# The second layer of experts 1 to 7 by Strassen's seven block products, interleaved with those of the first layer

## The chip, the cores and the metric

The kernel runs on one core of a Trainium2 chip. The metric is the device time of one execution in microseconds; of several runs the median is given. Five engines work side by side, each through its own instructions in order: TensorE (PE), VectorE (DVE), ScalarE (ACT), GpSimd (POOL) and SyncE (SP). They meet through semaphores, which the tile framework sets wherever one engine reads or overwrites what another wrote.

## The reference

Sparse attention over B=4, H=8, S=768, D=64 (32 neighbouring keys and 24 block summaries for each query) gives x, 3072 tokens of 512 numbers. The change lies in the dense mixture of experts behind it:

```python
logits = x @ w_gate                              # N=3072, E=8
P = np.exp(logits - logits.max())
for _ in range(8):                               # Sinkhorn
    P /= P.sum(1, keepdims=True) + 1e-09
    P /= P.sum(0, keepdims=True) + 1e-09
    P *= N / E
for e in range(E):                               # D=512, F=1024
    h = np.maximum(x @ w1[e], 0.0)
    out += P[:, e:e+1] * (h @ w2[e])
```

## The kernel before

**Stage 1** (pool `attn`) computes the attention, the gate, all of expert 0 and the Sinkhorn iterations. A planner, `Plan`, lays it out: `add` gives it units of work with an engine, a cost, a priority and what they depend on, and it fixes the order in which they are issued. Expert 0 is cut into batches of half a sequence (384 tokens): eight tiles of the hidden layer (`hidden_mm`, L204, four matmuls of 384 columns each, bank `hps`), then three output tiles (`project_mm`, L209, eight matmuls of 512 columns each, bank `yps`). A Sinkhorn iteration is `sink_rows` (L492 to L496: row sums, reciprocals, multiplication, column sums, all on DVE), `sink_cols` (L502: a matmul that adds the column sums over the partitions) and `sink_apply` (L505, L506, DVE). Weights are loaded on POOL's DMA queue, `load_w1` and `load_w2`, 1 MB each and expert.

**Stage 2** (pools `fast` and `fps`) computes experts 1 to 7 in an order that is written out by hand. A step is an expert e and a slice j of 512 tokens out of each half of the 3072 (21 steps). Each step has four groups (i = 0 to 3; 84 in all).

The **first layer** of a group makes four tiles of 128 features by 512 tokens by the Strassen-Winograd scheme: two halves of features, two of the contraction, two of tokens, seven block products instead of eight. Each product is two matmuls of 512 columns (`product`, L807), with operands that are quarters of w1 (A11 to A22) and x (B11 to B22) or sums of them (S1 to S4 from `w_sum`, L787 to L796; T1 to T4 from `x_sums`, L772 to L775). p1 goes to bank `pa`, and ACT copies it to bank `pg` (L822, called the seed here); p6 adds to `pg`, p2 to `pa`. p5 goes to `pb`, and ACT copies it out (L828, c5), as it does `pg` after p6 (L833, c2). p3 adds to `pb`, p7 to `pg`, and `both` (L840, L841) adds c2 or c5 on DVE and takes the relu. p4 adds to `pg` at last. ACT takes the relu of p1+p2 and of the last state of `pg` (L195). The hidden tiles `hf` are half precision (FP16).

The **second layer** is plain: of the step before, each group makes two output tiles of 128 tokens (`out_tile`), eight matmuls of 512 columns each in a bank `yps` (L209), and DVE adds the tile times its column of P to `out_acc` (L871). For expert 1, `out_acc`, which holds expert 0's output, is first multiplied by expert 0's column of P (L860). SP stores a tile after expert 7.

So a group is 14 matmuls of the first layer and 16 of the second, all 512 columns wide, each with a weight load of its own. p4 of a group is issued only after p1 and p5 of the next (`late`). The four groups of the first step have no second layer beside them and run two at a time; the fifth group is the first of the steady part. After the last group its step's eight output tiles remain alone, 64 matmuls.

Of the kernel before, what the change touches and what calls it, by code (L numbers as in the profile page):

```python
# [113 lines left out]
def kernel(  # L114
# [38 lines left out]
    ident = const.tile([128, 128], BF16)  # L153
    ident16 = const.tile([128, 128], FP16)
    band = const.tile([128, LIVE], BF16)
    m_blk = const.tile([128, G, 64], BF16)
    col_en = const.tile([128, 128], FP32)
    warm = const.tile([1, 8], FP32)
    zeros = const.tile([128, 512], BF16)
# [11 lines left out]
    def band_constants():  # L171

        nc.gpsimd.affine_select(out=band, in_=band, compare_op=ALU.is_ge, fill=0.0,
                                base=-1, pattern=[[1, LIVE]], channel_multiplier=-1)
        nc.gpsimd.affine_select(out=band, in_=band, compare_op=ALU.is_ge, fill=0.0,
                                base=2 * W - 1, pattern=[[-1, LIVE]], channel_multiplier=1)


    w1s, w2s = {}, {}

    def load_w1(e, part=0, parts=1):
        if part == 0:
            w1s[e] = wpool.tile([128, KD, F], FP16, tag="w1", name="w1")
        fw = F // parts
        nc.gpsimd.dma_start(  # L185
            out=w1s[e][:, :, part * fw:(part + 1) * fw],
            in_=moe_w1[e].rearrange("(dk p) f -> p dk f", p=128)[:, :, part * fw:(part + 1) * fw])
# [14 lines left out]
    def hidden_mm(e, hp, t0, n, f):  # L202
        for dk in range(KD):
            nc.tensor.matmul(hp[:, 0:n], lhsT=w1s[e][:, dk, f * 128:(f + 1) * 128],  # L204
                             rhs=xT[:, dk, t0:t0 + n], start=(dk == 0), stop=(dk == KD - 1))
# [12 lines left out]
    with tc.tile_pool(name="attn", bufs=1) as attn, \  # L218
         tc.tile_pool(name="aps", bufs=1, space=PSUM) as aps, \
         tc.manual_schedule():  # L220

        qT = [attn.tile([128, W + S + W], BF16, name=f"qT{i}") for i in range(NB)]
# [268 lines left out]
        def sink_rows():  # L491
            nc.vector.tensor_reduce(out=rs_sb[:], in_=P_sb[:], axis=AX.X, op=ALU.add)  # L492
            nc.vector.reciprocal(out=rrec_sb[:, :, 0], in_=rs_sb[:])
            nc.vector.tensor_tensor(out=P_sb[:], in0=P_sb[:],
                                    in1=rrec_sb[:].to_broadcast([128, NT, E]), op=ALU.mult)
            nc.vector.tensor_reduce(out=csum_sb[:], in_=P_sb[:].rearrange("p t e -> p e t"),  # L496
                                    axis=AX.X, op=ALU.add)

        def sink_cols():

            at["sink"] = bank("a", "sink")[:, 0:E]
            nc.tensor.matmul(at["sink"], lhsT=col_en, rhs=csum_sb[:], start=True, stop=True)  # L502

        def sink_apply(last):
            nc.vector.reciprocal(out=crec_sb[:, 0, :], in_=at.pop("sink"))  # L505
            nc.vector.scalar_tensor_tensor(out=P_sb[:], in0=P_sb[:], scalar=1.0 / XS if last else 1.0,  # L506
                                           in1=crec_sb[:].to_broadcast([128, NT, E]),
                                           op0=ALU.mult, op1=ALU.mult)

        def hidden0(key, t0, f):  # L510
            if f == 0:
                at["h", key] = hpool.tile([128, KF, 512], FP16, tag="h", name="h")
            hp = at["hp"] = bank("m", "hps")
            hidden_mm(0, hp, t0, HS, f)
            return hp
# [6 lines left out]
        def keep_busy(n):  # L522

            t = bank("m", "idle")
            for _ in range(n):
                nc.tensor.matmul(t[:], lhsT=zeros[:, 0:128], rhs=zeros[:], start=True, stop=True)  # L526
# [4 lines left out]
        for t in v_x:  # L531
            nc.vector.memset(t[:, :, :, D:VD], 1.0 / XS)

# [139 lines left out]
        def expert0(t0, xs):  # L673
# [3 lines left out]
            w = [U["w1", 0], U["w1", 1]]  # L677
# [39 lines left out]
        load(("w1", 0), lambda: load_w1(0, 0, 2), 0.85, 2.5)  # L717
        load(("w1", 1), lambda: load_w1(0, 1, 2), 0.85, 2.5)
# [11 lines left out]
        for i in range(PB, NP):  # L730
# [3 lines left out]
            if i % PB == PB - 1:  # L734
# [4 lines left out]
                expert0(b * S + HS, xs)  # L739
        load("w1n", lambda: load_w1(1), 0.85, 5.0)  # L740
# [14 lines left out]
    with tc.tile_pool(name="fast", bufs=1) as fast, \  # L755
         tc.tile_pool(name="fps", bufs=1, space=PSUM) as fps, \
# [5 lines left out]
        FH = F // 2  # L762
        steps = [(e, j) for e in range(1, E) for j in range(NJ)]
        xTs = fast.tile([128, 4, KH, NH], FP16, name="xTs")
        ws = {}
        hs = {}

        def x_sums(j):
            a, b = slice(512 * j, 512 * (j + 1)), slice(NH + 512 * j, NH + 512 * (j + 1))
            lo, hi = xT[:, 0:KH, :], xT[:, KH:KD, :]  # L770
            t = [xTs[:, n, :, a] for n in range(4)]
# [111 lines left out]
        for j in range(NJ):  # L883
            x_sums(j)
# [70 lines left out]
```

## Time and profile before

| | us |
|---|---|
| three runs: median, lowest, highest | 720.6, 720.39, 722.2 |
| the profiled execution | 721.05 |
| its span in the trace | 719.3 |

The profile is of one execution, on the hardware. In the rows, "L209" is a line of the code above, "x8" so many instructions of the same kind on end, "out<-in" the tiles written and read, followed by the shape. In the chain of waits and the timeline a row starts with its time from the span's start and its length; square brackets hold the engine's idle time before it and the instruction that ended it. Matmuls are pipelined, so a row's length is more than its cost on PE, which is the distance from one start to the next. The granted clock is TensorE's, as a share of full speed (1.00 throughout here).

### The profile page before, as it was taken

What the parts mean: (1) busy time and instruction counts of PE and PEld (TensorE: products, weight loads), DVE (VectorE), ACT (ScalarE), POOL (GpSimd) and SP (SyncE); (2) the same over time, 40 slices, a digit from 0 to 9 for tenths busy, and PEclk for the clock granted to TensorE, in tenths of its full rate; (3) what the DMA queues carried; (4) which work ended last, traced back from release to release, by engine and by line L of the source; (5) the groups of instructions that cost most, each with busy time, mean ns of one, the idle gap of its engine ahead of it and who ended that gap; (6) DMA issues with size and microseconds to landing.
All of it is one profiled execution on the core that took longest, in us unless ns stands there. A gap on an engine that the chain in (4) does not pass through costs nothing.

```text
span 719.3 us, 10589 instructions
## 1 busy us (share of the span) xinstructions
PE 704.5 (98%) x4182; PEld 341.0 (47%) x4186; DVE 422.1 (59%) x922; ACT 328.6 (46%) x596; POOL 86.4 (12%) x112
## 2 busy tenths in 40 slices
PE   8999999799999999999999999999999999999997
PEld 4666665453444444444444444444444444444443
DVE  6878887852666655554555455544555455544553
ACT  4677776456434433444334433444334433444330
POOL 9599700000000000000000000000000000000000
PEclk9999999999999999999999999999999999999999
DMA  9999960007000340030301230033003120001223
GB/s 133 177 130 127 132 97 3 1 1 117 1 1 0 60 59 0 1 59 7 52 1 19 40 60 0 1 60 58 1 0 59 13 47 1 1 0 60 78 83 132
DMA packets 86609, 33.70 MB, mean 47 GB/s; under 512 B 68640, under 2 KB 79904, under 8 KB 86560
## 3 DMA queue, kind: packets, MB, share of 16 engines
q0 software_dynamic: 77968, 26.22, 33.6%
q1 hardware_dynamic: 8064, 6.80, 3.1%
q8 instruction: 33, 0.54, 0.3%
q14 instruction: 16, 0.13, 0.1%
q10 hardware_dynamic: 528, 0.02, 0.0%
HBM read 52.45 MB, written 6.29 MB: 82 GB/s over the span
## 4 chain that ended last, share of the span: by engine, by line
PE 95%; DVE 4%; issue 0%; ACT 0%; DVEq 0%
PE yps L209 46%; PE pg L807 15%; PE pa L807 10%; PE pb L807 10%; PE hps L204 5%; PE sg L297 1%; PE tkq L278 1%; PE idle L526 1%; PE ss L383 1%; PE vs L305 1%; PE tx L469 1%; PE av L431 1%; DVE hf L840 1%; PE av L369 1%; PE av L375 1%
## 5 line engine op out<-in xcount | busy, mean ns | idle before, releaser
L209 PE MATMUL yps<-w,hf 128*128 128x512 f16 x1344 | 329.4, 379 | 0.0
L871 DVE SCALAR_TENSOR_TENSOR out_acc<-yps,P_sb,out_acc 128x512 f32<-128x512 f32 x168 | 126.0, 750 | 237.4 <-PE yps L209 237.4
L209 PEld LDWEIGHTS <-hf 128*128 128x128 f16 x1344 | 131.5, 98 | 158.6
L822 ACT COPY pg<-pa 128x512 f32<-128x512 f32 x84 | 47.8, 571 | 259.9 <-PE pa L807 259.9
L807 PEld LDWEIGHTS <-ws 128*128 128x128 f16 x672 | 65.7, 98 | 79.3
L807 PE MATMUL pa<-xT,w 128*128 128x512 f16 x336 | 99.3, 379 | 0.1
L807 PE MATMUL pg<-xTs,ws 128*128 128x512 f16 x336 | 99.3, 379 | 0.0
L807 PEld LDWEIGHTS <-w 128*128 128x128 f16 x504 | 49.3, 98 | 63.6 <-issue 4.6
L833 ACT COPY c<-pg 128x512 f32<-128x512 f32 x84 | 49.1, 588 | 42.3 <-PE pg L807 42.3
L840 DVE TENSOR_TENSOR hf<-pb,c 128x512 f16<-128x512 f32 x84 | 57.2, 681 | 16.6 <-PE pb L807 16.5
L840 DVE TENSOR_TENSOR hf<-pg,c 128x512 f16<-128x512 f32 x84 | 57.4, 683 | 0.0
L195 ACT ACTIVATE hf<-pg 128x512 f16<-128x512 f32 x84 | 51.6, 614 | 9.2 <-PE pg L807 9.2
L807 PE MATMUL pg<-xTs,w 128*128 128x512 f16 x168 | 50.0, 379 | 3.5 <-DVE hf L840 3.5
L841 DVE TENSOR_SCALAR hf<-hf 128x512 f16<-128x512 f16 x168 | 49.4, 294 | 5.8
L195 ACT ACTIVATE hf<-pa 128x512 f16<-128x512 f32 x84 | 50.5, 604 | 0.0
L807 PE MATMUL pb<-xTs,ws 128*128 128x512 f16 x168 | 49.6, 379 | 0.0
L807 PE MATMUL pb<-xT,ws 128*128 128x512 f16 x168 | 49.6, 379 | 0.0
L828 ACT COPY c<-pb 128x512 f32<-128x512 f32 x84 | 49.5, 592 | 0.0
L185 POOL DMA_DIRECT2D w<-in_moe_w_dram x9 | 7.0, 786 | 353.3 <-PE pg L807 225.1
L204 PE MATMUL hps<-xT,w 128*128 128x384 f16 x256 | 47.2, 326 | 0.0
L209 PE MATMUL yps<-w,h 128*128 128x512 f16 x192 | 46.2, 379 | 0.0
L204 PEld LDWEIGHTS <-w 128*128 128x128 f16 x256 | 23.3, 99 | 15.2 <-issue 1.5
(110 smaller groups left out, 531.4 us busy)
## 6 DMA issues: line engine op xcount, KB each, us to landing
w<-in_moe_w_dram POOLq DMA_DIRECT2D x15, 1024.0 KB, 8.6
out_dram<-out_acc SPq DMA_DIRECT2D x24, 256.0 KB, 2.0
vx<-in_v_dram POOLq DMA_DIRECT2D x32, 96.0 KB, 5.1
kst<-in_k_dram POOLq DMA_DIRECT2D x24, 96.0 KB, 4.5
qst<-in_q_dram POOLq DMA_DIRECT2D x24, 96.0 KB, 4.2
w<-in_moe_w_dram POOLq DMA_DIRECT2D x2, 512.0 KB, 8.5
kst<-in_k_dram POOLq DMA_DIRECT2D x4, 192.0 KB, 4.6
qst<-in_q_dram POOLq DMA_DIRECT2D x4, 192.0 KB, 4.9
```

The source lines that it names most:

```text
L195: nc.scalar.activation(out=out, in_=in_, func=AF.Relu, bias=0.0, scale=1.0)
L204: nc.tensor.matmul(hp[:, 0:n], lhsT=w1s[e][:, dk, f * 128:(f + 1) * 128], rhs=xT[:, dk, t0:t0 + n], start=(dk == 0), stop=(dk == KD - 1))
L209: nc.tensor.matmul(yp[:], lhsT=h[:, f, c * 128:(c + 1) * 128], rhs=w2s[e][:, f, :], start=(f == 0), stop=(f == KF - 1))
L278: nc.tensor.transpose(t[:, g * 128:(g + 1) * 128], st[:, g, :, :].rearrange("p j d -> p (j d)"), ident)
L297: nc.tensor.matmul(dst, lhsT=kT[r][p0:p0 + 64, g * 128:(g + 1) * 128], rhs=qT[r][p0:p0 + 64, g * 128 + l0:g * 128 + l1], start=True, stop= ...
L807: nc.tensor.matmul(bank[:], lhsT=weight(e, a, dk, i), rhs=moving(b, dk, j), start=start and dk == 0, stop=dk == KH - 1, skip_group_check=True)
L822: nc.scalar.copy(out=G["g"][:], in_=G["a"][:])
L828: nc.scalar.copy(out=G["c5"][:], in_=G["b"][:])
L833: nc.scalar.copy(out=G["c2"][:], in_=G["g"][:])
L840: nc.vector.tensor_tensor(out=hb[:, f, :], in0=bank[:], in1=c[:], op=ALU.add)
L841: nc.vector.tensor_scalar_max(out=hb[:, f, :], in0=hb[:, f, :], scalar1=0.0)
L871: nc.vector.scalar_tensor_tensor(out=out_acc[:, t, :], in0=yp[:], scalar=P_sb[:, t, e:e + 1], in1=out_acc[:, t, :], op0=ALU.mult, op1=ALU.add)
```

## The change

**Second layer.** `pair(e, j, c)` makes the two output tiles ta (of the first half of the tokens) and tb (of the second) by seven block products as well, q1 to q7, with four matmuls of 256 columns each (`product2`, L811): the halves are those of tokens, of the 1024 features and of the 512 output columns. The bank tile `xy` holds four accumulators of 256 columns, 0 to 3. q1 goes to 0 and ACT copies it out (L918, c1); q5 goes to 1; DVE adds both into 2 (v5); q6 adds to 2 and ACT copies that to 3 (L930, v6); q2 adds to 0, q7 to 2, q3 to 3, q4 to 1. Then DVE adds 0 and 3, times P, to tile ta (ya, L948), and 1 and 2 to tile tb (yb, L948). The left half of tb is kept as a difference; `fin` undoes it for expert 7, and a POOL subtraction behind `scale0` sets it up for expert 1.

**Its operands.** The hidden tile of a group is now `hf` [128, 7, 512]: A11, A12, A22, S1, S2, S4 and one place that holds first A21 and then S3. c12 and c22 are the sums of bank and copy that `both` made (L757), r12 and r22 their relus (L866, L869), r11 and r21 the relus on ACT (L187); s1, s3, s2, s4 are four new sums on DVE (L757, L754). The sums of w2 (`w2_sum`, three tiles and one in place) are made a piece at a time; so are those of w1 (`w1_sums`, one set for each e and i, with S3 in place of A21). w1 comes in four pieces of two DMAs. T3 is made in place of part of x.

**Order.** The second layer runs four groups behind the first (`LAG = 4`). On PE a group is q1, p1, p5, q5, p2, p6, q6, p3, p7, q2, q4, q3, p4, q7. The buffers c5 and c2 go from two to one each. After the last group four pairs remain, 112 matmuls, two of them with banks of the first layer for their accumulators.

**Moved.** The Sinkhorn iterations (`sinkhorn()`) and the second half of expert 0's last batch (`rest_of_0()`) go from stage 1 into the first groups of stage 2, where `route()` and `filler()` call them. Sinkhorn's two multiplications go from DVE to POOL (L988, L1000). `scale0`, expert 0's scaling, goes from DVE to ACT (L903).

```diff
-    hpool = ctx.enter_context(tc.tile_pool(name="hpool", bufs=2))
-    mps = ctx.enter_context(tc.tile_pool(name="mps", bufs=3, space=PSUM))
...
-        prev = [U["lo", b] for b in range(B)]
-        for n in range(8):
-            rows = add("DVE", 1.65, sink_rows, prev, 0)
-            buf = Buffer("a")
-            cols = add("PE", 0.1, sink_cols, [rows], 0, opens=[buf], lag=0.1)
-            prev = [add("DVE", 0.6, lambda n=n: sink_apply(n == 7), [cols], 0, uses=[buf])]
...
+        def w2_sum(e, n):
             if n == 0:
+                ws2[e] = extra[0].tile([128, 3, FH, DH], FP16, tag="ws2", name="ws2", bufs=2)
+            m = {w: moving2(w, e) for w in "B11 B12 B21 B22 T1 T2 T3 T4".split()}
+            sub(*[m[w] for w in (("T1", "B12", "B11"), ("T2", "B22", "T1"), ("T3", "B22", "B12"),
+                                 ("T4", "T2", "B21"))[n]])
...
+        def product2(e, c, bank, a, b, start):
+            w = moving2(b, e)
+            for f in range(FH):
+                nc.tensor.matmul(bank, lhsT=a(f)[:, 128 * c:128 * (c + 1)], rhs=w[:, f, :],
+                                 start=start and f == 0, stop=f == FH - 1, skip_group_check=True)
...
+            h = hs[e, j, i] = fast.tile([128, 7, 512], FP16, tag="hf", name="hf", bufs=8)
...
+            def s1():
+                plus(h[:, S1, :], h[:, A21, :], h[:, A22, :])
+            def s3():
+                sub(h[:, S3, :], h[:, A11, :], h[:, A21, :])
+            def s2():
+                sub(h[:, S2, :], h[:, S1, :], h[:, A11, :])
+            def s4():
+                sub(h[:, S4, :], h[:, A12, :], h[:, S2, :])
...
+        def pair(e, j, c, spare=False, c1_at=None):
...
+            def scale0():
+                for t in (ta, tb):
+                    nc.scalar.activation(out=out_acc[:, t, :], in_=out_acc[:, t, :], func=AF.Copy,
+                                         scale=P_sb[:, t, 0:1])
+                nc.gpsimd.tensor_tensor(out=out_acc[:, tb, 0:DH], in0=out_acc[:, tb, DH:DM],
+                                        in1=out_acc[:, tb, 0:DH], op=ALU.subtract)
...
+            def v5():
+                plus(at(2), at(1), B["c1"])
+            def q6():
+                product2(e, c, at(2), h(S2), "T2", False)
+            def v6():
+                nc.scalar.copy(out=at(3), in_=at(2))
...
+        def sinkhorn():
+            for n in range(8):
+                nc.vector.tensor_reduce(out=rs_sb[:], in_=P_sb[:], axis=AX.X, op=ALU.add)
+                nc.vector.reciprocal(out=rrec_sb[:, :, 0], in_=rs_sb[:])
+                nc.gpsimd.tensor_tensor(out=P_sb[:], in0=P_sb[:],
+                                        in1=rrec_sb[:].to_broadcast([128, NT, E]), op=ALU.mult)
+                yield
+                nc.vector.tensor_reduce(out=csum_sb[:], in_=P_sb[:].rearrange("p t e -> p e t"),
+                                        axis=AX.X, op=ALU.add)
+                yield
+                t = fps.tile([128, 4, DH], FP32, tag="xy", name="sink", bufs=2)
+                nc.tensor.matmul(t[:, 0, 0:E], lhsT=col_en, rhs=csum_sb[:], start=True, stop=True)
+                yield
...
+            do("q1", "p1")
+            do0("r21")
+            do("c1", "seed")
+            route()
+            do0("ya", "yb")
+            do("p5", "c5")
+            filler()
+            route()
+            do("q5", "v5")
+            do0("s4", "fin")
+            do("p2", "r11")
+            if j == 2 and i > 1 and later:
+                w1_sums(e + 1, i - 2)
...
+            do("p6", "c2")
+            filler()
+            route()
+            do("q6", "v6")
+            do("p3", "c12")
+            route()
+            do("p7", "c22", "r12")
+            route()
+            do("q2", "q4", "q3")
+            filler()
+            do("r22", "s1", "s3", "p4", "s2", "q7")
+            route()
```

These are DVE's instructions of one group in the steady part of the kernel before: the two times `both`, and the accumulations of two output tiles.

```order
L840 TENSOR_TENSOR hf_4807<-pb_4865,c2_4880 128x512
L841 TENSOR_SCALAR hf_4807<-hf_4807 128x512
L840 TENSOR_TENSOR hf_4807<-pg_4863,c5_4868 128x512
L841 TENSOR_SCALAR hf_4807<-hf_4807 128x512
L871 SCALAR_TENSOR_TENSOR out_acc_83<-yps_4898,P_sb_78,out_acc_83 128x512
L871 SCALAR_TENSOR_TENSOR out_acc_83<-yps_4921,P_sb_78,out_acc_83 128x512
```

The same stretch of DVE's work in the changed kernel, from one pair's accumulations on, in a group with four w1 sums:

```order
L948 SCALAR_TENSOR_TENSOR out_acc_74<-xy_6869,P_sb_69,out_acc_74 128x512 x2
L757 TENSOR_TENSOR xy_6941<-xy_6941,c1_6950 128x256
L754 TENSOR_TENSOR hf_6868<-hf_6868 128x512
L757 TENSOR_TENSOR ws1_6970<-w1_6589 128x256
L754 TENSOR_TENSOR ws1_6970<-ws1_6970,w1_6589 128x256
L754 TENSOR_TENSOR w1_6589<-w1_6589 128x2x128
L754 TENSOR_TENSOR ws1_6970<-w1_6589,ws1_6970 128x256
L757 TENSOR_TENSOR hf_6940<-pb_6956,c2_6977 128x512
L757 TENSOR_TENSOR hf_6940<-pg_6952,c5_6959 128x512
L866 TENSOR_SCALAR hf_6940<-hf_6940 128x512
L869 TENSOR_SCALAR hf_6940<-hf_6940 128x512
L757 TENSOR_TENSOR hf_6940<-hf_6940 128x512
```

Where six instructions stood, there are now the accumulations as one row of two, the sum v5 (`xy<-xy,c1`), s4 of the group before, four w1 sums (in some groups one w2 sum, in others none), c12 and c22, two relus and s1; s3 and s2 follow behind the last row.

On ACT, these are the copies and relus of a group in the steady part of the kernel before.

```order
L822 COPY pg_4074<-pa_4071 128x512
L828 COPY c5_4079<-pb_4076 128x512
L195 ACTIVATE hf_4021<-pg_4026 128x512
L833 COPY c2_4091<-pg_4074 128x512
L195 ACTIVATE hf_4021<-pa_4071 128x512
```

The changed kernel has these on ACT in a group, from r21 of the group before on:

```order
L187 ACTIVATE hf_5017<-pg_5029 128x512
L918 COPY c1_5095<-xy_5086 128x256
L824 COPY pg_5097<-pa_5091 128x512
L832 COPY c5_5104<-pb_5101 128x512
L187 ACTIVATE hf_5085<-pa_5091 128x512
L839 COPY c2_5119<-pg_5097 128x512
L930 COPY xy_5086<-xy_5086 128x256
```

Before, c2 (`c2<-pg`) is ahead of the group's first relu (`hf<-pa`); after, that relu (r11) is ahead of c2, and c1 and v6 are new.

Last, DVE where stage 2 begins: before, the Sinkhorn rows (`rs_sb` to `crec_sb`) run among the sums of x (`xTs`).

```order
L492 TENSOR_REDUCE rs_sb_79<-P_sb_78 128x24
L772 TENSOR_TENSOR xTs_2876<-xT_77 128x2x512
L493 RECIPROCAL rrec_sb_80<-rs_sb_79 128x24
L773 TENSOR_TENSOR xTs_2876<-xT_77,xTs_2876 128x2x512
L494 TENSOR_TENSOR P_sb_78<-P_sb_78,rrec_sb_80 128x192
L774 TENSOR_TENSOR xTs_2876<-xT_77 128x2x512
L496 TENSOR_REDUCE csum_sb_81<-P_sb_78 128x8
L775 TENSOR_TENSOR xTs_2876<-xT_77,xTs_2876 128x2x512
L505 RECIPROCAL crec_sb_82<-sink_2598 128x8
```

In the changed kernel the rows of an iteration run among the first groups' sums (`hf`, `ws1`):

```order
L997 RECIPROCAL crec_sb_73<-sink_2824 128x8
L757 TENSOR_TENSOR ws1_2846<-w1_1825 128x256
L754 TENSOR_TENSOR ws1_2846<-ws1_2846,w1_1825 128x256
L754 TENSOR_TENSOR w1_1825<-w1_1825 128x2x128
L754 TENSOR_TENSOR ws1_2846<-w1_1825,ws1_2846 128x256
L986 TENSOR_REDUCE rs_sb_70<-P_sb_69 128x24
L987 RECIPROCAL rrec_sb_71<-rs_sb_70 128x24
L991 TENSOR_REDUCE csum_sb_72<-P_sb_69 128x8
L754 TENSOR_TENSOR hf_2778<-hf_2778 128x512
L997 RECIPROCAL crec_sb_73<-sink_2873 128x8
```

The multiplications of P_sb are gone from DVE's row (they are POOL's now), and between one iteration's reciprocal of `sink` and its next row sums there can stand the sums of w1 for a whole group.

More of the change, by code (lines that the diff above doesn't have):

```diff
@@ L489, in logits_out @@
                 in_=at.pop(("lp", b)), func=AF.Exp, bias=0.0, scale=1.0 / XS)
[L491 to L508, printed above, removed]
         def hidden0(key, t0, f):
             if f == 0:
-                at["h", key] = hpool.tile([128, KF, 512], FP16, tag="h", name="h")
+                at["h", key] = hpool.tile([128, KF, HS], FP16, tag="h", name="h")
             hp = at["hp"] = bank("m", "hps")
@@ L855, in group @@
[L855 to L872 removed]
+                product1(e, i, j, B["g"], "A22", "T4", False)
@@ L873, in second, with store, ya @@
                                                op0=ALU.mult, op1=ALU.add)
+            def store(t, k=slice(0, DM)):
+                nc.sync.dma_start(out=out[t * 128:(t + 1) * 128, k], in_=out_acc[:, t, k])
+            def ya():
+                add(ta, 0, 0, 3)
                 if e == E - 1:
-                    nc.sync.dma_start(out=out[t * 128:(t + 1) * 128, :], in_=out_acc[:, t, :])
-            return first, second
-        for _ in range(2):
-            t = fps.tile([128, 512], FP32, tag="g", name="pg", bufs=2)
-            nc.tensor.matmul(t[:], lhsT=zeros[:, 0:128], rhs=zeros[:], start=True, stop=True)
```

434 lines of the change are left out of this document (286 added, 148 removed).

## The prediction

> **What bounds the kernel now.** First the page's busy times, then the busy times by stretch (columns: length, then PE, PEld, DVE, ACT, POOL busy with instruction counts, granted clock, DMA share, GB/s).
>
> ```profile
> PE 704.5 (98%) x4182; PEld 341.0 (47%) x4186; DVE 422.1 (59%) x922; ACT 328.6 (46%) x596; POOL 86.4 (12%) x112
> ```
>
> ```profile
> 130.00:140.00 10.00, 7.09 (x63) 4.21 (x62) 10.00 (x25) 4.27 (x10) 0.00 (x0) 1.00 0.01 2
> ...
> 180.00:190.00 10.00, 8.25 (x39) 3.61 (x37) 6.81 (x15) 3.35 (x7) 0.00 (x0) 1.00 0.01 2
> ...
> 600.00:700.00 100.00, 100.00 (x465) 45.37 (x464) 52.75 (x98) 40.94 (x77) 0.00 (x0) 1.00 0.10 38
> ```
>
> From 190 us on PE never pauses, at full clock, while DVE works 53% and ACT 41% of the time. Before that, where attention ends and the experts begin, PE waits. The chain of waits (start, length, what) shows the period of the steady part, and PE's timeline the step of one matmul:
>
> ```profile
> 187.68 1.73 PE yps L209 x8
> ...
> 699.21 1.73 PE yps L209 x8
> 701.37 13.83 PE yps L209 x64
> ```
>
> ```profile
> 122.77 0.50 PE L469 MATMUL tx<-ident,xs 128*128 128x128 f16 x6
> 123.10 2.75 PE L209 MATMUL yps<-w,h 128*128 128x512 f16 x12
> ...
> 158.12 3.41 PE L204 MATMUL hps<-xT,w 128*128 128x384 f16 x20
> 161.37 5.34 PE L209 MATMUL yps<-w,h 128*128 128x512 f16 x24
> ...
> 166.55 0.38 PE L880 MATMUL pg<-zeros 128*128 128x512 bf16 x1
> ```
>
> A group takes (699.21 - 187.68)/79 = 6.475 us. From start to start, 24 matmuls of 512 columns take 166.55 - 161.37 = 5.18 us, 0.2158 each; 20 of 384 take 3.25 us, 0.1625 each; 6 of 128 take 0.33 us, 0.055 each. That is 0.416 ns a column and 2.6 ns a matmul, every one with weights of its own. 30 x 0.2158 = 6.474: the period is PE's issue time and nothing else.
>
> **Term 1: PE's work in a group.** 16 matmuls of 512 columns become 28 of 256; 14 stay. One of 256 columns costs 0.1625 - 128 x 0.000416 = 0.109 us. The new group is 14 x 0.2158 + 28 x 0.1092 = 6.08 us.
>
> The Trainium skill ("TensorE: Matmul & The Clock Gate", Back-to-back issue gap) says that in a real stream of loads and matmuls the step is set by both, about 81 ns at 128 columns, not 56. Its 25 ns on each narrow matmul would, as an estimate, make the group 6.08 + 28 x 0.025 = 6.78 us; the row of 55 ns at 128 columns disagrees.
>
> **Term 2: new waits in a group.** How ACT and DVE answer PE, and what they take:
>
> ```profile
> 409.40 0.59 PE L807 MATMUL pa<-xT,w 128*128 128x512 f16 x2
> 409.83 0.59 PE L807 MATMUL pb<-xTs,ws 128*128 128x512 f16 x2
> 410.08 0.57 ACT L822 COPY pg<-pa 128x512 f32<-128x512 f32 x1 [3.29 <-PE pa L807]
> 410.57 0.59 ACT L828 COPY c<-pb 128x512 f32<-128x512 f32 x1
> ```
>
> ```profile
> 130.07 0.68 DVE L788 TENSOR_TENSOR ws<-w 128x1024 f16<-128x1024 f16 x1
> 130.68 0.68 DVE L790 TENSOR_TENSOR ws<-w,ws 128x1024 f16<-128x1024 f16 x1
> ...
> 173.00 0.68 DVE L840 TENSOR_TENSOR hf<-pg,c 128x512 f16<-128x512 f32 x1
> 173.72 0.29 DVE L841 TENSOR_SCALAR hf<-hf 128x512 f16<-128x512 f16 x1
> 173.93 0.68 DVE L840 TENSOR_TENSOR hf<-pg,c 128x512 f16<-128x512 f32 x1
> ```
>
> ```profile
> 173.74 0.59 PE L807 MATMUL pg<-xTs,w 128*128 128x512 f16 x2 [1.41 <-DVE hf L840]
> ```
>
> ```profile
> L871 DVE SCALAR_TENSOR_TENSOR out_acc<-yps,P_sb,out_acc 128x512 f32<-128x512 f32 x168 | 126.0, 750 | 237.4 <-PE yps L209 237.4
> L195 ACT ACTIVATE hf<-pa 128x512 f16<-128x512 f32 x84 | 50.5, 604 | 0.0
> L195 ACT ACTIVATE h<-hps 128x384 f16<-128x384 f32 x49 | 24.0, 491 | 12.4 <-PE hps L204 11.9
> L462 DVE TENSOR_TENSOR xs<-av,rc 128x384 f16<-128x384 f32 x32 | 17.8, 558 | 1.1
> L346 DVE TENSOR_TENSOR em<-er,band 128x768 bf16<-128x768 bf16 x24 | 12.8, 550 | 1.5 <-ACT er L340 1.5
> ```
>
> ACT starts 0.25 us after the last issue of a product (409.83 to 410.08) and its next instruction 0.49 after that; PE goes on 0.06 us after the release (173.68 to 173.74). DVE instructions that don't need each other overlap by 0.08 us (0.68 long, 0.61 apart); one that needs the last starts 0.04 after it (173.68 to 173.72).
>
> PE's new group, by start: q1 0, p1 0.44, p5 0.87, q5 1.30, p2 1.74, p6 2.17, q6 2.60, p3 3.04, p7 3.47, q2 3.90, q4 4.34, q3 4.78, p4 5.21, q7 5.65. What each has to wait for:
> - p2 writes over p1's bank, so the seed copy must be out: 0.87 + 0.25 + 0.57 + 0.06 = 1.75. It is 0.01 late.
> - p7 writes over p6's bank, so c2 must be out. The relu r11 now stands ahead of it on ACT (2.18 + 0.25 = 2.43), so c2 starts at 2.92 and frees the bank at 2.92 + 0.59 + 0.06 = 3.57, where p7 is due at 3.48: 0.09 to 0.10 late, and all that is queued behind p7 with it. Before, c2 stood ahead of the relu, with projection matmuls in between, and cost nothing.
> - q6 needs v5, the new DVE sum from PSUM to PSUM. No row has one of 256 columns; 384 to 512 columns (0.558, 0.682) put it at 0.43, with 0.68 as the upper end. 1.75 + 0.25 + 0.43 + 0.06 = 2.49 against 2.61: hidden; at 0.68 q6 would be 0.13 late. Nothing suggests a gain.
> - p4 needs c22: 3.73 + 0.60 + 0.68 + 0.06 = 5.07 against 5.31, and q2 needs v6 (0.38 from the two relu rows): 3.41 + 0.38 + 0.06 = 3.85 against 4.00. Both hidden.
>
> DVE, start to start: two accumulations 0.67 each, v5 0.35, two PSUM sums 0.60, two relus 0.21 and 0.33, four half-precision sums of 512 columns 0.34 each (0.42 long, by the step from 768 to 1024 columns, 0.55 to 0.68): 4.8 us, plus 0.92 for the four first-layer weight sums or 0.61 for one second-layer sum in 8 groups of 12. That is 4.8 to 5.7 of 6.19 us: DVE is nearly full but not late. ACT has 3.1 us, and 1.0 more in the twelve groups where it now does DVE's scaling of expert 0's rows, after v6 and ahead of p4's relu, where it has room; the POOL subtraction behind it is awaited only by yb a group later. The weight loads come two groups ahead of their sums (12 us, where 1 MB lands in 8.6) on POOL, which PE does not wait for.
>
> ```profile
> w<-in_moe_w_dram POOLq DMA_DIRECT2D x15, 1024.0 KB, 8.6
> ```
>
> So a group takes 6.08 + 0.10 + 0.01 = 6.19 us, between 6.08 (c2 in time) and 6.35 (v5 late as well). 79 groups x (6.475 - 6.19) = 22.5 us gained.
>
> **Term 3: the filling of the pipeline.** The Sinkhorn iterations and half of expert 0's last batch move into the first four groups.
>
> ```profile
> 130.60 2.76 PE L204 MATMUL hps<-xT,w 128*128 128x384 f16 x16
> 134.40 0.36 PE L502 MATMUL sink<-csum_sb,col_en 128*128 128x8 f32 x2 [1.04 <-DVE csum_sb L496]
> ...
> 139.46 0.36 PE L502 MATMUL sink<-csum_sb,col_en 128*128 128x8 f32 x2 [1.88 <-DVE csum_sb L496]
> ...
> 189.25 0.59 PE L807 MATMUL pa<-xT,w 128*128 128x512 f16 x2
> ```
>
> ```profile
> 152.62 0.21 DVE L505 RECIPROCAL crec_sb<-sink 128x8 f32<-128x8 f32 x1 [0.91 <-PE sink L502]
> ...
> 153.98 0.36 DVE L494 TENSOR_TENSOR P_sb<-P_sb,rrec_sb 128x192 f32<-128x192 f32 x1
> 154.38 0.50 DVE L496 TENSOR_REDUCE csum_sb<-P_sb 128x8 f32<-128x192 f32 x1
> 155.36 0.21 DVE L505 RECIPROCAL crec_sb<-sink 128x8 f32<-128x8 f32 x1 [0.48 <-PE sink L502]
> ```
>
> Before, group 5 starts at 189.25. Now the attention stage, without Sinkhorn waits and the moved half, has 44 x 0.1625 + 48 x 0.2158 = 17.5 us of matmuls after 133.2: it ends at 150.7. Then DVE, not PE, sets the pace, since each sink matmul waits for DVE's csum and the group's products are queued behind it: four groups' sums 4 x 3.1, eight iterations of Sinkhorn 8 x 1.4 (0.39 + 0.33 + 0.45 + 0.21, start to start), token and weight sums 9.2 (2 x 2.45, 2 x 0.92, 2.5), together 32.8 us, against 22.5 on PE. Each iteration also goes to POOL twice for the multiplication that DVE did in 0.36. No POOL row has it; I take 0.5 us and 0.2 for the hops, between 0.36 and 1.0: 16 x 0.7 = 11.2, of which, laid out by hand along DVE's order, some 4.5 stand bare; the rest runs beside other sums. DVE begins 3.3 after the stage's start and is through at 150.7 + 3.3 + 32.8 + 4.5 = 191.3; v5, then q6 to q7 of group 4 follow (3.9): group 5 starts at 195.2, 5.9 us later than before. Bounds: 189 (8 iterations of 2.74 us, all else hidden) and 202 (every multiplication bare).
>
> The Trainium skill ("GPSIMD Engine Reference", Elementwise) gives about 2.6 cycles an element there; as an estimate that is 0.57 us, and the sum would rise by at most 1.1 us.
>
> **Term 4: the end.** 64 matmuls (13.8 us) become 112 narrow ones (12.2), with perhaps 0.5 of waits, and p4 no longer trails its group (0.4): 1.5 us gained. After the last matmul a sum, a scaled addition and the store remain, as now:
>
> ```profile
> 715.22 0.75 DVE L871 SCALAR_TENSOR_TENSOR out_acc<-yps,P_sb,out_acc 128x512 f32<-128x512 f32 x1 [0.98 <-PE yps L209]
> ```
>
> **Sum.** -22.5 + 5.9 - 1.5 = -18.1 us. The profiled execution took 721.05 us with a span of 719.3; the median of the runs is 720.6, 0.45 below it. 721.05 - 18.1 - 0.45 = 702.5 us.
>
> **Rivals.** Break-even is a group of 6.42 us, 0.23 above 6.19.
> - DVE sets the pace, slower than before. If its instructions stood end to end (0.68 + 0.68 + 2 x 0.29 + 4 x 0.42 + 0.43 + 2 x 0.75 = 5.55, weight sums 0.6 on average, some 14 gaps of 0.04), a group would take 6.7 us and the kernel 702.5 + 79 x 0.51 = 743. For it: nine more DVE instructions a group, each in order, several waiting for ACT and PE. Against: the overlap of 0.08 in the rows. It decides from 6.42 us of DVE a group. Chance 0.07, with smaller delays of the same kind from 723 on.
> - The narrow matmuls pay for their weight loads, also slower: from 0.23/28 = 8 ns each on the gain is gone, at 25 ns it is 702.5 + 79 x 0.7 + 112 x 0.025 = 761 (what the skill's figure would make of it). Against it, 55 ns at 128 columns. Chance 0.02.
> - The gain is eaten: 0.1 more wait in a group and 8 us more in the filling, 718.5 to 723. In-order waits on three engines make this possible, no row shows it. Chance 0.05.
> - The full gain: c2 in time and a filling no longer than before, 702.5 - 8.7 - 5.9 = 688. Chance 0.10.
>
> **How the numbers follow.** The forecast, 690 to 716 (6.35 a group is +12.6, the filling -6 to +7), has 0.76. The range 689 to 717 leaves out the slow rivals and half of the full gain. A measurement can tell 0.3% (2.2 us) from no change. Faster: 0.76 + 0.10 = 0.86; within 0.3%: 0.05; slower: 0.09.
>
> **What would show it.** Right: narrow matmuls 0.109 us apart; a group of 6.15 to 6.25 us whose only repeated PE wait is p7 on ACT's c2; DVE 80 to 95% busy; group 5 starting at 190 to 202 us, with PE waiting for the csum before. Wrong: a period over 6.4, PE waiting at q6 or p4 for DVE in every group, or narrow matmuls over 0.117 us apart.

## The result, and the profile after

The changed kernel takes 704.03 us (median of three runs, 704.01 to 705.0) where the kernel before takes 720.6: a ratio of 0.9768, 95% interval 0.9743 to 0.9793. The profiled execution took 704.03 us with a span of 702.3, 17.0 less than before. Forecast were 702.5 us and a fall of 18.1 us.

The page's busy times, and then stretches of the profile (length, PE, PEld, DVE, ACT and POOL busy with their counts, granted clock, DMA share, GB/s):

```profile
PE 681.3 (97%) x5192; PEld 440.2 (63%) x5192; DVE 587.4 (84%) x1433; ACT 406.3 (58%) x788; POOL 141.3 (20%) x189
```

```profile
170.00:180.00 10.00, 6.04 (x23) 2.36 (x21) 6.67 (x16) 3.05 (x6) 1.88 (x3) 0.83 0.00 0
180.00:190.00 10.00, 6.01 (x26) 2.32 (x25) 8.02 (x21) 3.16 (x6) 2.46 (x4) 0.89 0.00 0
190.00:200.00 10.00, 10.00 (x53) 5.92 (x54) 8.89 (x21) 5.70 (x11) 2.99 (x4) 0.77 0.01 2
...
300.00:400.00 100.00, 100.00 (x689) 67.02 (x687) 90.90 (x215) 56.16 (x116) 10.92 (x15) 1.00 0.27 30
```

In the steady part PE is still busy all the time and DVE now 91% of it. The filling, 170 to 200 us, shows idle PE and, which was not forecast, a granted clock of 0.77 to 0.89. PE's timeline there and in one steady group, with the ACT instructions around c2:

```profile
174.02 0.42 PE L995 MATMUL sink<-csum_sb,col_en 128*128 128x8 f32 x2 [3.13 <-DVE csum_sb L991]
174.28 1.01 PE L805 MATMUL pa<-xT,w 128*128 128x512 f16 x2
175.09 1.06 PE L805 MATMUL pg<-xTs,ws 128*128 128x512 f16 x2
...
186.38 0.39 PE L995 MATMUL sink<-csum_sb,col_en 128*128 128x8 f32 x2 [3.48 <-DVE csum_sb L991]
...
191.12 1.06 PE L811 MATMUL xy<-w,hf 128*128 128x256 f16 x4
...
198.53 1.04 PE L811 MATMUL xy<-w,hf 128*128 128x256 f16 x8
```

```profile
409.87 0.59 PE L805 MATMUL pa<-xT,w 128*128 128x512 f16 x2
...
410.73 0.60 PE L811 MATMUL xy<-ws,hf 128*128 128x256 f16 x4
411.17 0.59 PE L805 MATMUL pa<-xT,w 128*128 128x512 f16 x2
...
411.80 0.60 ACT L187 ACTIVATE hf<-pa 128x512 f16<-128x512 f32 x1 [0.23 <-PE pa L805]
...
412.29 0.58 ACT L839 COPY c<-pg 128x512 f32<-128x512 f32 x1
...
412.47 0.59 PE L805 MATMUL pb<-xT,ws 128*128 128x512 f16 x2
...
412.93 0.59 PE L805 MATMUL pg<-xT,w 128*128 128x512 f16 x2
...
415.97 0.59 PE L805 MATMUL pa<-xT,w 128*128 128x512 f16 x2
...
416.04 1.41 DVE L948 SCALAR_TENSOR_TENSOR out_acc<-xy,P_sb,out_acc 128x512 f32<-128x512 f32 x2
...
678.27 0.59 PE L805 MATMUL pa<-xT,w 128*128 128x512 f16 x2
...
683.49 1.04 PE L811 MATMUL xy<-w,hf 128*128 128x256 f16 x8
```

q5 takes 411.17 - 410.73 = 0.44 us for four narrow matmuls, 0.109 each; the group takes 415.97 - 409.87 = 6.10. Over 44 groups, (678.27 - 409.87)/44 is 6.100 too.

The prediction counts the groups from 0: its group 4 is the first with a second layer, its group 5, at 189.25 in the kernel before, the first of the 79 that it sums up. (The expectations further down count from 1.) In the changed kernel group 4 begins with q1 at 191.12, and the row at 198.53 holds its q7 and q1 of group 5, which is at 198.53 + 0.44 = 198.97; the row at 683.49 likewise puts the end of the last group at 683.93. One row of the timeline of the kernel before is added, the start of its tail:

```profile
701.20 13.98 PE L209 MATMUL yps<-w,hf 128*128 128x512 f16 x64
```

| | before | after | measured, us | forecast |
|---|---|---|---|---|
| start of group 5 | 189.25 | 198.97 | +9.7 | +5.9 |
| 79 groups | 511.95 (6.480 each) | 484.96 (6.139 each) | -27.0 | -22.5 |
| the rest, to the span's end | 18.1 | 18.4 | +0.3 | -1.5 |
| span | 719.3 | 702.3 | -17.0 | -18.1 |

So 27.0 us are gained in the groups, and 9.7 given back while the pipeline fills.

### The profile page after: what moved, and what is told of

It reads as the page before. It is cut to its first block, busy times and chain, and to the rows that moved or that the text cites. A ratio compares the mean times of both kernels' runs of the same rounds, so it can differ in the third digit from the quotient of the medians.

```text
span 702.3 us, 13621 instructions
## 1 busy us (share of the span) xinstructions
PE 681.3 (97%) x5192; PEld 440.2 (63%) x5192; DVE 587.4 (84%) x1433; ACT 406.3 (58%) x788; POOL 141.3 (20%) x189
## 4 chain that ended last, share of the span: by engine, by line
PE 85%; DVE 12%; issue 2%; ACT 0%; POOL 0%; DVEq 0%; POOLq 0%; ACTq 0%
PE xy L811 32%; PE pg L805 13%; PE pb L805 9%; PE pa L805 9%; PE hps L196 5%; PE yps L201 5%; DVE hf L757 3%; DVE out_acc L948 2%; PE sg L296 1%; PE idle L506 1%; PE tkq L277 1%; DVE hf L866 1%; DVE hf L754 1%; PE ss L382 1%; PE vs L304 1%
## 5 line engine op out<-in xcount | busy, mean ns | idle before, releaser
L811 PEld LDWEIGHTS <-hf 128*128 128x128 f16 x2352 | 230.2, 98 | 100.1 <-issue 6.4
L811 PE MATMUL xy<-w,hf 128*128 128x256 f16 x1312 | 183.8, 273 | 0.0
L811 PE MATMUL xy<-ws,hf 128*128 128x256 f16 x984 | 148.1, 273 | 1.5
L187 ACT ACTIVATE hf<-pg 128x512 f16<-128x512 f32 x84 | 50.2, 597 | 160.8 <-PE pg L805 160.8
L948 DVE SCALAR_TENSOR_TENSOR out_acc<-xy,P_sb,out_acc 128x512 f32<-128x512 f32 x164 | 115.2, 744 | 1.7 <-PE xy L811 1.7
L754 DVE TENSOR_TENSOR hf<-hf 128x512 f16<-128x512 f16 x252 | 98.8, 420 | 2.9
L757 DVE TENSOR_TENSOR hf<-pb,c 128x512 f16<-128x512 f32 x84 | 58.1, 691 | 40.7 <-ACT xy L930 32.3
L172 POOL DMA_DIRECT2D w<-in_moe_w_dram x56 | 42.4, 835 | 186.8 <-PE pg L805 181.3
L805 PEld LDWEIGHTS <-ws 128*128 128x128 f16 x504 | 49.6, 98 | 43.1 <-issue 1.6
L187 ACT ACTIVATE hf<-pa 128x512 f16<-128x512 f32 x84 | 50.2, 597 | 26.6 <-PE pa L805 26.3
L757 DVE TENSOR_TENSOR hf<-pg,c 128x512 f16<-128x512 f32 x84 | 57.2, 681 | 0.0
L805 PE MATMUL pg<-xTs,ws 128*128 128x512 f16 x168 | 50.4, 382 | 0.0
L805 PE MATMUL pg<-xT,w 128*128 128x512 f16 x168 | 50.2, 380 | 0.2 <-ACT c L839 0.2
L918 ACT COPY c<-xy 128x256 f32<-128x256 f32 x82 | 30.5, 373 | 22.4 <-PE xy L811 22.4
```

What stands on the lines that cost most here:

```text
L172: nc.gpsimd.dma_start(out=t[:, :, h, :], in_=moe_w1[e].rearrange("(dk p) f -> p dk f", p=128)[:, :, f:f + 128])
L187: nc.scalar.activation(out=out, in_=in_, func=AF.Relu, bias=0.0, scale=1.0)
L754: nc.vector.tensor_tensor(out=out, in0=in0, in1=in1, op=ALU.subtract)
L757: nc.vector.tensor_tensor(out=out, in0=in0, in1=in1, op=ALU.add)
L805: nc.tensor.matmul(bank[:], lhsT=w[:, dk, :], rhs=x[:, dk, :], start=start and dk == 0, stop=dk == KH - 1, skip_group_check=True)
L811: nc.tensor.matmul(bank, lhsT=a(f)[:, 128 * c:128 * (c + 1)], rhs=w[:, f, :], start=start and f == 0, stop=f == FH - 1, skip_group_check=True)
```

## The experiments

Each kernel below is the changed kernel with the edit shown. Unless an interval is given it was executed once, with the profiler, to be set beside 704.03 us and the span of 702.3.

**The twelve groups of expert 1.** In the groups that scale expert 0's rows the trace shows a period of 6.36 us instead of 6.10. DVE's and POOL's rows of one of them, and PE around q6:

```profile
248.64 0.72 POOL L905 TENSOR_TENSOR out_acc<-out_acc 128x256 f32<-128x256 f32 x1 [5.64 <-ACT out_acc L903]
248.66 0.85 DVE L866 TENSOR_SCALAR hf<-hf 128x512 f16<-128x512 f16 x1
...
250.23 0.59 PE L805 MATMUL pa<-xT,w 128*128 128x512 f16 x2
...
250.88 1.40 DVE L948 SCALAR_TENSOR_TENSOR out_acc<-xy,P_sb,out_acc 128x512 f32<-128x512 f32 x2
...
251.96 0.59 PE L805 MATMUL pg<-xTs,ws 128*128 128x512 f16 x2
...
252.20 0.42 DVE L757 TENSOR_TENSOR xy<-xy,c 128x256 f32<-128x256 f32 x1
...
252.68 0.60 PE L811 MATMUL xy<-ws,hf 128*128 128x256 f16 x4
...
256.59 0.59 PE L805 MATMUL pa<-xT,w 128*128 128x512 f16 x2
```

r12 starts 0.02 us after POOL's subtraction and takes 0.85 us; elsewhere it takes 0.28. All that DVE does after it is late by as much: ya and yb, then v5, and q6 starts 0.72 after p6 instead of 0.43. The next c12 waits for p3 behind that q6, so the delay comes round again: a ring of waits, v5, q6, p3, c12, c22, r12, r22, s1, s3, s2, ya, yb, v5. Its steps, from one start to the next, add up to 0.48 + 0.43 + 0.70 + 0.61 + 0.60 + 0.20 + 0.32 + 0.46 + 0.67 + 1.32 = 5.79 us without POOL (the seven from p3 to ya are 412.47 to 416.04 in the steady group above), and to 6.36 with the 0.57 that r12 loses.

```diff
-                nc.gpsimd.tensor_tensor(out=out_acc[:, tb, 0:DH], in0=out_acc[:, tb, DH:DM],
-                                        in1=out_acc[:, tb, 0:DH], op=ALU.subtract)
+            def split0():
+                sub(out_acc[:, tb, 0:DH], out_acc[:, tb, DH:DM], out_acc[:, tb, 0:DH])
...
             do0("s4", "fin")
+            if q and groups[n - LAG][0] == 1:
+                do("split0")
```

> In the twelve groups that handle expert 1's output a group took 6.36 us instead of 6.10, and in each of them r12 on DVE took 0.85 us instead of 0.28 while POOL's subtraction (0.72 us) ran. Theory: POOL's subtraction holds DVE's half-precision instruction up, and that lengthens a ring of waits (v5, q6, p3, c12, c22, relus, sums, ya, yb, v5) from 5.79 to 6.36. Here the subtraction is done on DVE, ahead of the scaling and outside the ring (behind s4). Then r12 takes 0.28 again, these groups take 6.10 to 6.15, and the span falls by about 3 us, from 702.3 to 699.3. Rival: ACT's two scalings (1.33 us a group) make these groups long; then they stay at 6.36 and the span at 702.3 or above.

Measured: 701.3 us, span 699.6, 2.7 less.

```profile
248.20 0.59 PE L805 MATMUL pa<-xT,w 128*128 128x512 f16 x2
...
252.99 0.28 DVE L866 TENSOR_SCALAR hf<-hf 128x512 f16<-128x512 f16 x1
...
254.42 0.59 PE L805 MATMUL pa<-xT,w 128*128 128x512 f16 x2
```

r12 is back at 0.28 with ACT's scalings unchanged: the rival falls. This group, with four w1 sums, takes 6.22, a little more than expected; that DVE now has the subtraction too may be why. The Trainium skill ("SBUF — State Buffer", Who interferes with whom) says that DVE and GpSimd share a pair of ports as an exclusive lock, so that a DVE instruction in a two-port mode waits for the whole of a GpSimd instruction that began first. By that, as an estimate, r12 would have taken 0.98 us (the 0.70 that POOL had left and its own 0.28); 0.85 comes near it. No run here shows which mode r12 runs in.

**The low clock in the filling.**

```diff
+                for _ in range({4: 13, 6: 15}.get(n, 0)):
+                    nc.tensor.matmul(t[:, 2:4, :].rearrange("p k d -> p (k d)"), lhsT=zeros[:],
+                                     rhs=zeros[:, None, :].to_broadcast([128, 4, 128]), start=True, stop=True)
                 nc.tensor.matmul(t[:, 0, 0:E], lhsT=col_en, rhs=csum_sb[:], start=True, stop=True)
```

> In the filling PE waited 3.13 and 3.48 us for csum, and some 2 us after each wait its matmuls of 512 columns were 0.43 us apart instead of 0.216 (granted clock 0.83, 0.89 and 0.77 in 170 to 200 us). Here 13 and 15 matmuls of zeros, which nothing reads, stand ahead of the two sink matmuls that waited so long, so that PE is busy meanwhile. Theory: the clock falls because PE was idle for 3 us; then it stays at 1.00, the first of the two slow stretches (1.6 us longer than at full clock, DVE waiting for pb) is saved and the second is hidden behind DVE: span 700.6. Rival: the clock falls for another reason; then it is as low as before and the span is 702.3 or up to 1 us above it.

Measured: 701.82 us, span 700.1, 2.2 less. The stretches of this kernel:

```profile
170.00:180.00 10.00, 8.85 (x43) 3.98 (x42) 7.92 (x19) 2.53 (x6) 2.19 (x4) 1.00 0.00 0
180.00:190.00 10.00, 8.53 (x41) 3.69 (x39) 8.43 (x22) 4.29 (x9) 2.17 (x4) 1.00 0.01 2
```

The clock stays at 1.00. Some 0.5 of the 2.2 us was there before the first of these waits (the sink matmul ahead of it starts at 166.09 here and at 166.59 in the changed kernel), so the low clock cost about 1.7 us. That PE's idleness lowered the clock fits this, but one execution does not settle it. The kernel with the sums outside the ring, further down, is the same program in the filling, has the same waits (3.13 and 3.47 us) and no matmuls of zeros, and in its execution the clock stayed at 1.00 too:

```profile
183.45 0.39 PE L995 MATMUL sink<-csum_sb,col_en 128*128 128x8 f32 x2 [3.47 <-DVE csum_sb L991]
```

```profile
180.00:190.00 10.00, 4.61 (x23) 2.16 (x24) 8.74 (x22) 4.24 (x9) 2.42 (x4) 1.00 0.01 2
```

Of the seven profiles here that have both waits of over 3 us, it is the only one with a full clock in the filling; the three whose waits there are 1.5 us at most (with matmuls of zeros, with Sinkhorn in stage 1, and the joined kernel) all have it. So the low clock came after long waits, but not after each of them. The Trainium skill ("TensorE: Matmul & The Clock Gate", What's actually happening) says that the clock is halved after an idle window of about 3.4 us, and that these windows run freely. The waits of 3.13 and 3.48 us are about as long, and a window that does not begin with the wait leaves room for the execution that kept its clock; no run here shows the windows themselves.

**The order on ACT**, which the prediction blamed for p7's wait.

```diff
-            do("p2", "r11")
+            do("p2")
...
             do("q6", "v6")
+            do("r11")
```

> ACT takes c2 and v6 ahead of r11. p3 to p7 was 0.46 us where two matmuls of 512 columns take 0.432, so p7 was 0.024 us late. Theory: that is the wait for c2 behind r11; with c2 first the group falls from 6.10 to 6.076 in the 68 groups after expert 1, 1.6 us in all, span 700.7; the twelve groups of expert 1 stay at 6.36. Rival: the 0.024 us belong to the issue of p7 and not to a wait; then the group stays at 6.10 and the span at 702.3. If r11 now comes too late for s3, a group gets longer than 6.10.

Measured: 705.85 us, span 704.1. The steady group stays at 6.10:

```profile
413.16 0.59 PE L805 MATMUL pg<-xTs,ws 128*128 128x512 f16 x2
...
413.84 0.59 ACT L839 COPY c<-pg 128x512 f32<-128x512 f32 x1 [0.71 <-PE pg L805]
414.02 0.59 PE L805 MATMUL pb<-xT,ws 128*128 128x512 f16 x2
...
414.48 0.59 PE L805 MATMUL pg<-xT,w 128*128 128x512 f16 x2
```

p3 to p7 is still 0.46, though ACT now stood idle for 0.71 us before c2: r11 did not hold c2 up (c2 starts 0.68 us after p6 here, 0.69 in the changed kernel). Yet p7 starts 0.05 us after c2's end (413.84 + 0.59). The way from p6 over c2 to p7 takes 414.48 - 413.16 = 1.32 us, and the matmuls in between 1.30: I put the 0.024 us down to that, which no run tested. Of the 1.8 us lost, 0.8 came in the filling: group 4 begins at 191.88 instead of 191.12. The granted clock was lower there, 0.73 in 180 to 190 us instead of 0.89, so this loss can't be put down to the order. Expert 1's groups, where r11 now stood behind v6, took 6.39 instead of 6.36, 0.4 us in all; the rest lies in four later groups of 6.19 to 6.38.

**What stands behind PE.** Three kernels, two with useless sums and one without q4.

```diff
             do("r22", "s1", "s3", "p4", "s2", "q7")
+            if n >= 16:
+                for _ in range(2):
+                    plus(scratch[:], xT[:, 0, 0:512], xT[:, 1, 0:512])
```

> Two useless half-precision sums of 512 columns (0.34 us each, start to start) are added on DVE in each of the last 68 groups, between s2 and the accumulations ya and yb, that is inside the ring of waits v5, q6, p3, c12, c22, r12, r22, s1, s3, s2, ya, yb, next v5, which adds up to 5.79 us in the trace of the changed kernel. Ring theory: the ring becomes 5.79 + 0.68 = 6.47 us, a group goes from 6.10 to 6.47 although DVE has only some 5.5 us of work in most groups, and the span from 702.3 to about 727. Busy-time theory: a group stays at 6.10 while DVE's work fits in; only the twenty or so groups with four w1 sums (6.4 us of DVE) grow by 0.3: span about 708.

The next has the same lines behind `do0("s4", "fin")`.

> The same two useless sums in the same 68 groups, but behind s4, outside the ring, where DVE waits up to 1 us for c12. Ring theory: groups without weight sums stay at 6.10, those with w1 sums grow by 0.3: span about 708, nearly 20 us below the kernel with the sums inside the ring. Busy-time theory: the place makes no difference, both kernels take the same.

And this one has:

```diff
-            do("q2", "q4", "q3")
+            do("q2", *(["q4"] if n < 16 else []), "q3")
```

> Leaves out q4, four narrow matmuls, in the last 68 groups (the right half of the second tile then lacks a product). If PE's issue alone sets the group: 6.10 - 4 x 0.109 = 5.66 us, span 702.3 - 68 x 0.44 = 672.6. If the ring of 5.79 us stands right behind PE: the group falls to 5.79 only, span 681.

Measured: spans of 735.5 (inside), 713.4 (outside) and 692.5 (without q4). The place decides: the same two sums cost 33 us inside the ring and 14 outside. (The span shows 11 for the second, but there group 5 began at 195.98 instead of 198.97, ahead of all these sums: 1.25 us of this were there before PE's long waits, the rest goes with the clock, which stayed at 1.00.) Inside, the ring is what PE waits for (start, length, and in brackets the wait):

```profile
413.95 0.88 DVE L757 TENSOR_TENSOR scratch<-xT 128x512 f16<-128x512 f16 x2
...
414.75 1.40 DVE L948 SCALAR_TENSOR_TENSOR out_acc<-xy,P_sb,out_acc 128x512 f32<-128x512 f32 x2
...
416.54 0.60 PE L811 MATMUL xy<-ws,hf 128*128 128x256 f16 x4 [0.35 <-DVE xy L757]
```

The two sums take 0.80 and not 0.68, so the ring is 6.59, and 68 groups of 0.49 make the 33 us. But the kernel without q4 refutes that the ring stands next behind PE: its groups take 5.95, not 5.79. Its rows show what does:

```profile
409.61 0.59 PE L805 MATMUL pb<-xT,ws 128*128 128x512 f16 x2
...
410.92 0.68 DVE L757 TENSOR_TENSOR hf<-pg,c 128x512 f16<-128x512 f32 x1
...
411.65 0.59 PE L805 MATMUL pg<-xTs,w 128*128 128x512 f16 x2
...
412.95 0.60 PE L805 MATMUL pa<-xT,w 128*128 128x512 f16 x2
...
418.90 0.60 PE L805 MATMUL pa<-xT,w 128*128 128x512 f16 x2
```

p4 writes the bank that c22 reads, and starts 0.05 us after c22's end (410.92 + 0.68). From p3's start over c12 and c22 to p4 the way takes 0.70 + 0.61 + 0.73 = 2.04 us (409.61 to 411.65); p3, p7, q2, q4 and q3 give it 2.17 to 2.20. So only some 0.15 us of q4's 0.44 could be had. The sums outside the ring run against the same wait. There the groups without sums of weights stay at 6.10, as forecast; those with one w2 sum take 6.28 and those with four w1 sums 6.61 instead of the 6.4 forecast, hence 713.4 and not 708. PE's waits in 300 to 600 us of that kernel (total, times, longest) hold

```profile
PE pg L805 <- DVE hf L757: 5.6, 16, 0.4
```

**Where Sinkhorn stands.** The iterations go back into stage 1, and, apart from that, only the multiplications back to DVE.

```diff
+        prev = [U["lo", b] for b in range(B)]
+        for n in range(8):
+            rows = add("DVE", 1.65, sink_rows, prev, 0)
...
-        sink, fill = sinkhorn(), rest_of_0()
+        sink, fill = iter(()), rest_of_0()
```

> The Sinkhorn iterations go back into stage 1, multiplications on DVE as in the kernel before; half of expert 0's last batch stays in the filling. Theory: the filling is long because PE's in-order queue waits for csum behind DVE's sums (10.9 us of waits and the low clock after them); with the iterations done by about 155 us, DVE's own sums (some 22 us) set the pace of the first four groups, group 5 starts at about 180 us instead of 191.1, and the span is 691 to 694. Rival: DVE's sums of the groups, weights and tokens fill the time anyway, or the waits come back in stage 1 (1.0 to 1.9 us an iteration, as before the change); then the span is 698 or more.

```diff
-                nc.gpsimd.tensor_tensor(out=P_sb[:], in0=P_sb[:],
+                nc.vector.tensor_tensor(out=P_sb[:], in0=P_sb[:],
```

> Sinkhorn stays among the first groups, but its two multiplications are done by DVE again. Theory: the filling is long because of where the iterations stand in the queues, not because POOL multiplies; DVE loses five waits of 0.77 us for POOL and gains sixteen instructions of 0.36 us, so the span stays within 2 us of 702.3. Rival: the sixteen trips to POOL (0.52 to 0.59 us each and the way there and back) are what costs; then the span falls by 5 us or more, to 697.

Measured: with Sinkhorn in stage 1, 693.91 us and a span of 692.1, 10.2 less; with the multiplications on DVE, 703.92 us and 702.1, no change. So the place of the iterations costs the time, not POOL's share in them. Stage 1 gets some 3.1 us longer (its last sink matmul is below; in the changed kernel its matmuls end at 150.90), and yet the first group with a second layer begins 10.3 us earlier, at 180.84 instead of 191.12:

```profile
153.99 0.39 PE L500 MATMUL sink<-csum_sb,col_en 128*128 128x8 f32 x2 [1.46 <-DVE csum_sb L495]
...
180.84 0.60 PE L835 MATMUL xy<-w,hf 128*128 128x256 f16 x4
```

About 2 of the 10 us are the low clock of the filling: here it stayed at 1.00, and in the kernel with the sums outside the ring, where it did so with Sinkhorn among the groups, this group begins at 187.81, 3.3 us earlier than in the changed kernel, 1.25 of them there before the waits.

**A version faster than both.** First the parts together:

> Sinkhorn back in stage 1, the subtraction on DVE outside the ring, c2 and v6 ahead of r11 on ACT, and the token sums of the second and third slice one at a time over the first eight groups. Sum of the parts measured: 692.1 for Sinkhorn in stage 1, 2.7 us less for the subtraction; the order on ACT gave nothing in the steady part (1.8 us more, in the filling). Theory: DVE's sums set the pace of the first groups, so 2.7 us of token sums less there bring some 2 us: span 687 to 688. Rival: the filling is bound elsewhere, and the spread brings nothing: 689.5 or more.

690.95 us, span 689.2: Sinkhorn and the subtraction add up (692.1 - 2.7 = 689.4), and spreading the token sums brought nothing. DVE was idle for 0.9 to 1.9 us at a time in these groups anyway. Then further edits, with the token sums spread and not:

```diff
             do("q5", "v5")
+            if n == LAG:
+                w2_sum(1, 1)
...
             do("r22", "s1", "s3", "p4", "s2", "q7")
             route()
-            filler()
...
-                for m in range(4):
-                    w2_sum(1, m)
+                w2_sum(1, 0)
...
-                    sub(out_acc[:, tb, 0:DH], out_acc[:, tb, DH:DM], out_acc[:, tb, 0:DH])
+                    (nc.gpsimd if c1_at is not None else nc.vector).tensor_tensor(
+                        out=out_acc[:, tb, 0:DH], in0=out_acc[:, tb, DH:DM], in1=out_acc[:, tb, 0:DH],
+                        op=ALU.subtract)
```

> Sinkhorn in stage 1, the subtraction on DVE outside the ring, token sums one at a time over eight groups, ACT's order as in the changed kernel, and three more edits: the pieces of expert 0 spread evenly, three in each of the first four groups, so that the fourth has some too; expert 1's w2 sums one at a time between group 5's instructions instead of four in a row ahead of its v5; the subtraction of the last pairs of the plain form on POOL. In the joined kernel PE waited 1.9 us in group 4 and 1.2 us in group 5. Theory: these edits save 2 to 3 us of 689.2: span 686 to 687.5. Rival: PE's waits only move elsewhere: 689 or more.

> The same as the kernel before it in this call, but with the token sums of the second and third slice four in a row, as in the changed kernel. If DVE's sums still set the pace of the filling, it is 2 to 3 us slower than the one with the sums spread; if DVE has idle time there, both take the same within 1 us.

Measured: 691.54 us (five runs, 689.68 to 692.64), ratio to the kernel before 0.959, interval 0.9564 to 0.9616; and 692.46 us, ratio 0.9602, interval 0.9576 to 0.9627. Spread or not is the same within 1 us. Against the single execution of the joined kernel no gain is shown, as the rival had it; the executions of each version lie 3 to 4.6 us apart, so a gain of 1 us could not be seen. In the first of the two PE's longest wait in the filling is now 2.0 us, for the w2 sum that q4 needs. The medians of both versions lie 1.6 to 1.8% below that of the changed kernel.

## Why the prediction was right, and where it was wrong

The time lay 1.5 us above the forecast, well inside the range, but the terms were off by more than that: the groups gained 4.5 us more than forecast, the filling cost 3.8 more and the end 1.8 more. That these errors all but cancel is luck. The mechanism held: the steady time is PE's issue time, narrow matmuls cost 0.109 us, and DVE, 91% busy, does not set the pace. None of the rivals on the slow side came true; of the full gain one half did (c2 all but in time), the other, a filling no longer than before, did not. The 81 ns at 128 columns of the Trainium skill ("TensorE: Matmul & The Clock Gate", Back-to-back issue gap), by which a group would have taken 6.78 us, does not show in this stream of loads and matmuls: 0.109 at 256 columns is what the trace of before gave.

- **Term 2, the group's waits: too large.** p7 was to be 0.10 late and was 0.03. "The relu r11 now stands ahead of it on ACT" was the step that failed. ACT took r11 0.20 us after p2's last issue (411.80 - 411.60), not 0.25, and c2 followed on time for p6; with c2 first nothing changed. p2's 0.01 did not show. So a group takes 6.10 and not 6.19.
- **The POOL subtraction** "is awaited only by yb a group later": true of semaphores, and not enough. It held up r12 and made eleven of the 79 groups some 6.36 us long; without it the kernel is 2.7 us faster. That a resource is awaited by nobody does not make it free.
- **Term 3, the filling: right in kind, too small.** Stage 1 ended at 150.9 (150.7 forecast), PE waited seven times for csum, 10.9 us in all, and DVE set the pace; but DVE came to group 4's v5 at 194.96 and not at 191.3, and group 5 followed 4.0 us later (3.9 forecast). DVE's waits between 155 and 195 us (total, times, longest) show what the sum left out:

```profile
DVE rs_sb L986 <- POOL P_sb L1000: 3.8, 5, 0.8
DVE hf L757 <- PE pb L805: 2.2, 1, 2.2
DVE hf L757 <- ACT h L187: 0.8, 2, 0.4
DVE csum_sb L991 <- POOL P_sb L988: 0.7, 1, 0.7
DVE crec_sb L997 <- PE sink L995: 0.6, 3, 0.3
```

The waits for POOL are 4.5 us, just the 4.5 taken as bare. The step that failed is the sum that ends in "150.7 + 3.3 + 32.8 + 4.5 = 191.3": it lets DVE wait for POOL alone, and puts DVE's waits for PE and ACT at nothing. They are 3.6 us, which is the miss of 3.7 (its own work in between came to 32.6, as forecast). Of them 1.6 us come with the halved clock: where it stayed at 1.00, the wait for `pb` was 0.6 instead of 2.2. POOL's multiplication was sized well (0.52 to 0.59 us in thirteen of the sixteen, 0.77 to 0.90 in the others, for the 0.5 taken); the estimate of 0.57 us from the Trainium skill ("GPSIMD Engine Reference", Elementwise) names no length of a cycle, so it can't be followed, and the sum did not use it. With the multiplications on DVE nothing was saved. The bounds of 189 to 202 held.
- **Term 4, the end: wrong in sign,** -1.5 forecast, +0.3 measured. "A sum, a scaled addition and the store remain, as now" failed: DVE comes to be the bound there. In the rows of the tail it works with pauses of 0.05 us at most from 691.20 on, and ends 2.4 us after PE (696.23 + 0.44), against 1.0 before:

```profile
696.23 0.60 PE L811 MATMUL px<-ws,hf 128*128 128x256 f16 x4
...
698.62 0.48 DVE L977 SCALAR_TENSOR_TENSOR out_acc<-px,P_sb,out_acc 128x256 f32<-128x256 f32 x1
```

Of the signs named for it, three came: the spacing of 0.109, DVE at 80 to 95%, PE waiting for csum before a group 5 that starts at 190 to 202 us (199.0). A fourth, p7 behind c2 as the only repeated wait outside expert 1, came at 0.03 us, and only the rows around c2 speak for it. The period, 6.10, lay just below the 6.15 to 6.25 named.

## What to carry to other kernels

Where one engine is full, the next limit is not the busiest other engine but the shortest slack in a ring of waits: add up the starts round each ring (here 5.79 us, and a shorter path with 0.15 us to spare) and see where a new instruction lands; the same two sums cost 33 us inside the ring and 14 outside. Work that is moved into the filling of a pipeline must not put the full engine's in-order queue behind a slow chain: Sinkhorn there cost 10 us, about 2 of them by the low clock that followed PE's waits.

## What was not expected of the hardware

- A half-precision relu on DVE took 0.85 us instead of 0.28 while POOL ran a 0.72 us subtraction on other data; a sum of w1 beside a Sinkhorn multiplication on POOL (at 159.93 us) took 0.69 instead of 0.28.
- After PE had been idle for 3.13 and 3.48 us, matmuls of 512 columns stood 0.41 to 0.43 us apart (0.81 us for the two from 174.28, 0.86 for the two from 191.97) instead of 0.216. With matmuls of zeros in the waits they did not; nor did they in one execution of the same filling without them. A wait of 1.99 us was followed by a granted clock of 0.83 (190 to 200 us) in the last version and by 1.00 in the one before it.
- ACT started r11 0.20 us after p2's last issue where the kernel before showed 0.25, with about the same shapes; with c2 ahead of r11, c2 started 0.25 us after p6's (413.16 + 0.43 to 413.84). Why was not tested.
